# A new order of all engines for an attention-plus-feed-forward kernel, and five zero products at its start

## The chip, the cores and the metric

The kernel runs on one core of one Trainium2 chip. The metric is the device time of one execution in microseconds (us); smaller is better. Three runs of the kernel before gave 214.08, 215.25 and 216.29 us, so its median is 215.25 us.

## What is computed

The first stage is attention with a sliding window of 96 keys, eight global keys and a linear bias (a slope for each head); the second stage is a feed-forward layer with `h - tanh(h)` between its two products.

```python
# q, k, v: (4, 8, 768, 64) float32; n_global 8, n_local 96
scores = scale * np.matmul(q, k.transpose(0, 1, 3, 2))
is_global = pos[None, :] < n_global
is_local = (rel >= 0) & (rel < n_local)
dist = np.where(is_global & ~is_local, n_local, np.abs(rel))
scores = np.where(is_global | is_local, scores - slopes * dist, -1e9)
a = softmax(scores)                      # over the keys
x = (a @ v).transpose(0, 2, 1, 3).reshape(3072, 512)
h = x @ w_in                             # w_in 512 x 2048
out = (h - np.tanh(h)) @ w_out           # w_out 2048 x 512
```

## The kernel before

**Units.** The 3,072 rows are cut into 24 units of 128 queries (six to each of the four batches); one unit holds all eight heads. Units 0 to 3 are the first blocks of the four batches and see only their own 128 keys. Every later unit also needs the 128 keys before its own, and the eight global keys are copied into that block (`K` for the keys, `V` for the values).

**The order is written out by hand.** A long string `ORDER` (L17 to L65) lists all steps as words. Each word issues its instructions on one engine, and each engine runs its own words in the order of the string; nothing is reordered. A second string `HOMES` (L66 to L104) says which buffer or which of the eight PSUM banks each value lies in. A step waits for the data that it reads and for the last reader of the buffer that it writes, so both strings set the waits.

**The words of one unit u.** `lq.u`, `lk.u`, `lv.u` load q, k and v. For units 0 to 2, q and k come as float32: q over ACT's queue, k over SP's queue (`load_rows`, L292), and `cq.u`, `ck.u` cast them to bf16 on DVE (`/d`) or ACT (`/a`). All other loads go over POOL's queue. `T.u` transposes k and then q: on PE for units 0 to 6 (`a_T`, L305), with a copy from PSUM of each half (`Te.u.1` for k, `Te.u.0` for q, `a_Te`, L323); from unit 7 on as a DMA transpose issued by SP (`a_DT`, L332). `B.u` (only units 0 to 2) puts the bias and the mask into PSUM, two products of 512 columns (`bias`, L273). `S.n` are the score products (L347); from run 11 on, one `S` covers two blocks of one unit and one of a neighbour, so `S.11` needs the transposes of units 11 and 12. `E.u.o` is the exponential on ACT (L357), `M.u.o` the multiplication by the mask factors on DVE (L361), `AV.u` the product with v (L374), `R.u` the division by the row sum on DVE (L383), `X.u` the transpose of the result (PE for units 0 to 7, L394, with the copy `Xe.u`; later a DMA transpose by SP under the name `Xe.u`, L408).

**The masks.** DVE makes `dist`, `first` and `slopes` from an iota; `bm.m` are the products for the three masks (two of 512 columns each, L275) and `em.m` their exponential on ACT (L279).

**The feed-forward part.** Units are grouped: 0 and 1 alone, then three pairs (2 to 7), then four groups of four units. `m1.g.f` are the products with `w_in` for group g from chunk f on (L412), `th.g.f` the tanh on ACT, `g.g.f` the subtraction on DVE, `m2.u.c.a` a quarter of the products with `w_out` for unit u (L441), `ev.u` the copy of the result out of PSUM into one of four `ot` buffers (L450), and `st.u` the store (L453), on POOL's queue for units 0 to 20 and on SP's for the last three. `in.j` and `out.j` load the weights over POOL's queue: `in.0` and `in.1` two chunks of 128 columns each, `in.2` to `in.4` four each, `out.0` to `out.3` four chunks each.

**The helper `warm`** (L540) is one product of a zeroed tile with itself, 512 columns, into bank 7. The word `warm` does not occur in the order before, so no such product is issued.

The first words of PE in the order before are `bm.1 bm.0 B.1 T.1 B.0 T.0 S.1 T.3 B.2 S.0 T.2 S.3 AV.0 S.2 AV.1 X.0 T.4 X.1 AV.2 bm.2 m1.0.0 AV.3 X.2 m1.1.0 X.3 S.4`.

Of the kernel before, what the change touches and what calls it, by code (L numbers as in the profile page):

```python
# [17 lines left out]
lq.1 lk.1 zero rel ones.0 lq.0 lk.0 lq.3 slopes lq.2 lk.2 lk.3 dist table lv.0 turn bm.1 first ident lq.4 ones.1 bm.0  # L18
em.1 lk.4 cq.1/d ck.1/d B.1 lv.1 em.0 T.1 lv.2 B.0 cq.0/a ck.0/d in.1 Te.1.0/d Te.1.1/a T.0 in.0 S.1 Te.0.1/a Te.0.0/d
cq.2/a ck.2/d E.1.0 lv.3 T.3 B.2 in.2 Te.3.1/a Te.3.0/d S.0 lk.5 T.2 E.0.0 lq.5 S.3 Te.2.0/d Te.2.1/a AV.0 in.3 R.0  # L20
E.3.0 S.2 AV.1 out.0 X.0 R.1 E.2.0 T.4 out.1 M.3.0 X.1 Xe.0/a AV.2 bm.2 Te.4.1/d Xe.1/a out.2 m1.0.0 R.2 Te.4.0/a em.2
lv.4 AV.3 X.2 R.3 m1.1.0 Xe.2/a X.3 th.0.0 S.4 Xe.3/d th.1.0 in.4 g.0.0 m1.2.0 E.4.0 lk.6 g.1.0 m1.2.6 K.4 E.4.1 M.4.0
lq.6 m1.1.4 th.2.0 M.4.1 m1.2.2 th.1.4 g.2.0 m1.0.4 th.2.6 g.1.4 lv.5 th.2.2 T.5 g.2.6 m1.1.8 th.0.4 Te.5.0/d Te.5.1/a
g.0.4 m1.0.8 th.1.8 g.2.2 lq.10 S.5 th.0.8 g.1.8 m1.2.10 E.5.1 g.0.8 m1.2.8 K.5 th.2.10 M.5.1 m2.2.0.0 lv.6 E.5.0
g.2.10 m1.2.4 th.2.8 M.5.0 m2.1.0.0 g.2.8 th.2.4 m2.0.0.0 g.2.4 out.3 m2.2.0.1 lk.8 m2.2.0.2 m2.0.0.1 AV.4 lq.7
m1.1.12 V.4 lk.10 R.4 m1.2.14 th.1.12 lq.8 m1.0.12 g.1.12 th.2.14 lk.9 g.2.14 m1.2.12 th.0.12 lk.7 m2.1.0.1 g.0.12
th.2.12 lq.9 X.4 g.2.12 AV.5 Xe.4/a m2.1.0.2 R.5 T.6 V.5 lv.7 m2.0.0.2 Te.6.1/a Te.6.0/d lk.11 X.5 m2.2.0.3 Xe.5/a
m2.0.0.3 ev.2.0/a T.10 S.6 ev.0.0/a m1.3.10 T.8 E.6.1 K.6 m1.3.0 E.6.0 M.6.1 T.7 m1.3.2 th.3.10 M.6.0 m2.3.0.0 T.9
th.3.2 g.3.10 m1.3.4 th.3.0 g.3.2 m2.1.0.3 g.3.0 th.3.4 AV.6 g.3.4 ev.1.0/a m1.3.6 R.6 st.1.0 m1.3.12 lv.15 th.3.6 V.6
m2.3.0.1 g.3.6 lq.12 th.3.12 S.7 g.3.12 lv.8 m2.3.0.2 E.7.1 K.7 lv.17 m1.3.8 E.7.0 lk.13 M.7.1 X.6 m2.3.0.3 Xe.6/d  # L30
lv.10 th.3.8 M.7.0 S.8 ev.3.0/a st.0.0 g.3.8 AV.7 lv.9 E.8.1 m1.3.14 V.7 R.7 lq.11 E.8.0 m2.4.0.0 M.8.1 lq.18 X.7
th.3.14 m2.4.0.1 M.8.0 lk.12 Xe.7/a S.9 g.3.14 lq.13 AV.8 E.9.1 K.9 m2.4.0.2 lq.15 R.8 E.9.0 m1.4.6 lv.11 M.9.1 Xe.8
m2.4.0.3 M.9.0 th.4.6 lv.12 T.11 m1.4.8 g.4.6 ev.4.0/a S.10 T.12 th.4.8 AV.9 E.10.1 K.10 g.4.8 m1.4.0 T.13 R.9 E.10.0
m2.5.0.0 M.10.1 Xe.9 m1.4.4 th.4.0 V.9 M.10.0 m1.4.10 th.4.4 g.4.0 m2.5.0.1 th.4.10 g.4.4 AV.10 lq.14 g.4.10 m2.5.0.2
R.10 lv.16 m1.4.2 V.10 lv.13 Xe.10 S.11 th.4.2 lk.15 m2.5.0.3 g.4.2 E.11.0 lk.14 K.11 m1.4.12 K.12 ev.5.0/d E.11.1
st.4.0 m1.4.14 M.11.0 lk.17 th.4.12 M.11.1 m2.6.0.0 th.4.14 st.5.0 g.4.12 m2.6.0.1 E.12.0 g.4.14 AV.11 M.12.0 m2.7.0.0
R.11 m2.7.0.1 V.11 Xe.11 S.12 m2.7.0.2 T.15 E.12.1 m2.7.0.3 E.13.1 M.12.1 T.14 m2.6.0.2 ev.7.0/d E.13.0 AV.12 M.13.1
st.7.0 m2.6.0.3 lq.16 M.13.0 m1.5.7 R.12 ev.6.0/a lv.14 m1.5.6 th.5.7 V.12 Xe.12 lk.16 m1.5.1 g.5.7 th.5.6 lq.17 AV.13
g.5.6 th.5.1 lv.18 m1.5.3 R.13 lq.23 m1.5.0 th.5.3 g.5.1 Xe.13 lk.18 m1.5.11 g.5.3 th.5.0 m1.5.8 g.5.0 lq.19 th.5.11
S.13 g.5.11 lk.19 th.5.8 m1.5.4 g.5.8 E.14.0 T.16 K.14 m1.5.2 K.15 E.14.1 M.14.0 T.17 m1.5.9 th.5.4 M.14.1 m1.5.13  # L40
th.5.2 g.5.4 m1.5.14 E.15.0 g.5.2 m1.5.10 th.5.13 M.15.0 th.5.14 m1.5.5 g.5.13 T.18 th.5.10 g.5.14 m2.8.0.0 th.5.5
g.5.10 m1.5.15 th.5.9 g.5.5 AV.14 th.5.15 g.5.9 m2.8.0.1 T.19 V.14 R.14 m1.5.12 m2.8.0.2 g.5.15 Xe.14 th.5.12 S.14
g.5.12 m2.9.0.0 E.15.1 K.16 m2.8.0.3 E.16.0 M.15.1 m2.9.0.1 ev.8.0/d E.16.1 AV.15 M.16.0 st.8.0 m2.10.0.0 lv.19 R.15
m2.9.0.2 lk.23 V.15 Xe.15 M.16.1 S.15 lv.22 m2.9.0.3 E.17.1 K.17 lv.23 m2.10.0.1 ev.9.0/d E.18.0 st.6.0 m2.10.0.2
M.17.1 lq.22 E.17.0 M.18.0 m2.10.0.3 st.3.0 st.2.0 M.17.0 AV.16 lv.21 m2.11.0.0 V.16 T.23 R.16 lv.20 AV.17 m2.11.0.1
R.17 st.9.0 Xe.16 ev.10.0/a m2.11.0.2 lk.20 V.17 Xe.17 m1.6.0 st.10.0 lq.21 S.16 th.6.0 lq.20 m2.11.0.3 g.6.0 E.19.1
K.19 lk.21 m1.6.9 ev.11.0/d E.19.0 m1.6.6 M.19.1 th.6.9 M.19.0 m1.6.4 th.6.6 g.6.9 m1.6.3 E.18.1 lk.22 g.6.6 m1.6.15
th.6.4 M.18.1 th.6.3 AV.19 g.6.4 AV.18 th.6.15 g.6.3 m1.6.12 R.18 m1.6.2 th.6.12 V.19 Xe.18 m1.6.8 g.6.15 th.6.2 R.19
m1.6.7 th.6.8 g.6.12 Xe.19 m1.6.1 th.6.7 g.6.8 m1.6.11 th.6.1 T.20 g.6.7 m1.6.5 th.6.11 g.6.1 T.21 m1.6.10 g.6.11
th.6.5 g.6.2 m1.6.14 th.6.10 T.22 g.6.5 m1.7.12 th.6.14 g.6.10 m1.6.13 th.7.12 g.6.14 m1.7.1 g.7.12 th.6.13 m1.7.10  # L50
g.6.13 th.7.1 S.17 g.7.1 th.7.10 m2.13.0.0 g.7.10 E.21.0 K.21 m2.12.0.0 K.20 E.20.0 M.21.0 m2.13.0.1 E.20.1 M.20.0
m2.12.0.1 M.20.1 m2.13.0.2 AV.20 m1.7.14 V.20 R.20 m2.13.0.3 th.7.14 Xe.20 m1.7.9 g.7.14 ev.13.0/a m2.12.0.2 th.7.9
m2.12.0.3 g.7.9 S.18 ev.12.0/a m1.7.5 E.21.1 K.22 m2.14.0.0 E.22.0 M.21.1 m1.7.3 th.7.5 M.22.0 m1.7.2 th.7.3 g.7.5
# [13 lines left out]
mk.0:2,3 mk.1:0,1 mk.2:6,7 f32.0.k:3 kq.0:1 f32.0.q:2 f32.1.k:1 kq.1:0 f32.1.q:0 f32.2.k:5 kq.2:3 f32.2.q:4 v.0:0
v.1:1 kq.3:2 v.2:2 kq.4:4 v.3:3 v.4:4 kq.5:0 v.5:5 kq.6:1 v.6:6 kq.7:4 v.7:7 kq.8:3 v.8:9 kq.9:0 v.9:4 kq.10:2 v.10:11
kq.11:1 v.11:5 kq.12:2 v.12:6 kq.13:3 v.13:7 kq.14:1 v.14:9 kq.15:0 v.15:8 kq.16:3 v.16:0 kq.17:2 v.17:10 kq.18:4
v.18:4 kq.19:1 v.19:11 kq.20:2 v.20:7 kq.21:4 v.21:6 kq.22:3 v.22:5 kq.23:0 v.23:1 tr.0.0:1 tr.0.1:7 qk.0:1 s.0.0:2,3  # L70
p.0.0:1 av.0:2,3 x.0:0 xt.0:2 xT.0:0 tr.1.0:6 tr.1.1:0 qk.1:0 s.1.0:4,5 p.1.0:0 av.1:4,5 x.1:1 xt.1:1 xT.1:1 tr.2.0:4
tr.2.1:5 qk.2:3 s.2.0:6,7 p.2.0:3 av.2:4,5 x.2:2 xt.2:3 xT.2:2 tr.3.0:0 tr.3.1:1 qk.3:2 s.3.0:0,1 p.3.0:2 av.3:0,1
x.3:0 xt.3:5 tr.4.0:3 tr.4.1:0 qk.4:4 s.4.0:6,7 s.4.1:0,1 p.4.0:4 p.4.1:1 av.4:0,1 x.4:1 xt.4:0 xT.3:3 tr.5.0:7
tr.5.1:3 qk.5:5 s.5.0:0,1 s.5.1:6,7 p.5.0:3 p.5.1:0 av.5:4,5 x.5:2 xt.5:0 tr.6.0:7 tr.6.1:1 qk.6:6 s.6.0:4,5 s.6.1:0,1
p.6.0:1 p.6.1:2 av.6:4,5 x.6:0 xt.6:3 xT.4:1 qk.7:9 s.7.0:6,7 s.7.1:4,5 p.7.0:0 p.7.1:4 av.7:2,3 x.7:1 xt.7:6 qk.8:8
s.8.0:4,5 s.8.1:6,7 p.8.0:1 p.8.1:3 av.8:6,7 x.8:2 xT.5:0 qk.9:10 s.9.0:2,3 s.9.1:4,5 p.9.0:0 p.9.1:2 av.9:0,1 x.9:0
qk.10:7 s.10.0:6,7 s.10.1:2,3 p.10.0:1 p.10.1:4 av.10:0,1 x.10:1 qk.11:4 p.11.0:3 p.11.1:0 av.11:2,3 x.11:2 qk.12:5
# [30 lines left out]
def kernel(  # L108
# [11 lines left out]
    nc = tc.nc  # L120

    B, H, S, Dh = q.shape
    P = 128
# [352 lines left out]
    for u in range(NU):  # L476
        for j, (nm, src) in ((1, ("k", k)), (0, ("q", q))):
            if u < HW:
                h = ("f32", u, nm)
# [60 lines left out]
    def warm():  # L540
        nc.tensor.matmul(ps[:, 7, :], zero[:, 0, :], zero.to_broadcast([P, 4, P]), start=True, stop=True)

    done = set()
    with tc.manual_schedule(engines={PE, ACT, DVE, POOL, SP}):
        for word in ORDER.split():
            if word == "warm":
                warm()
                continue
# [40 lines left out]
```

## Time and profile before

| Quantity | Value |
|---|---|
| time, median of three runs | 215.25 us |
| time of the profiled execution | 215.35 us |
| its span, first to last instruction | 213.5 us |
| what lies around the span | 1.85 us |
| DVE busy | 130.4 us (61% of the span) |
| ACT busy | 120.5 us (56%) |
| POOL busy (mostly issuing DMAs) | 76.9 us (36%) |
| bytes moved by DMA | 27.55 MB, 129 GB/s on average |
| the product with `w_out` (L445) | 400 instructions, 91.2 us busy |
| the product with `w_in` (L420) | 576 instructions, 90.5 us busy |
| granted TensorE clock | 1.000 |

How to read it: an engine's busy time is the union of its instructions' times, without waits. The duration of one PE instruction includes its latency, and neighbours overlap in time, so a stretch of PE work is best read as the distance between starts. A line number is that of the instruction in the kernel; a helper such as the copy (L229 on ACT, L231 on DVE) serves many steps. A DMA's "landing" is counted from the issue to the last byte.

### The profile page before, as it was taken

The numbers are of one execution on the slowest core, as the hardware profiler recorded it, in microseconds if no ns is written. First come the engines' busy times: TensorE is split into PE (matmuls) and PEld (weight loads), VectorE is DVE, ScalarE is ACT, GpSimd is POOL, SyncE is SP. The second block draws the span as 40 slices with busy tenths as digits, with TensorE's granted clock in tenths as the row PEclk, the third lists the DMA queues.
The fourth block names the chain that finished last, engine by engine and source line by source line (L and its number), as shares of the span: only waits on it lengthen the run. The fifth ranks groups of instructions, "written<-read, shape, count | busy, mean of one in ns | idle before, by whom it ended". The sixth has DMA issues, their size and how long they took to land.

```text
span 213.5 us, 4492 instructions
## 1 busy us (share of the span) xinstructions
PE 204.6 (96%) x1796; PEld 117.2 (55%) x1796; DVE 130.4 (61%) x264; ACT 120.5 (56%) x179; POOL 76.9 (36%) x101
## 2 busy tenths in 40 slices
PE   4799999999999999999999999999999999999994
PEld 1467985857667665544555454444554444444442
DVE  7348883737787975789776498874567435611300
ACT  4579881557678474578445395673853335522422
POOL 8794435730995092780049830000010002002040
PEclk9999999999999999999999999999999999999999
DMA  5999999999999999999919999801021102002136
GB/s 164 243 177 189 208 198 175 179 157 194 128 177 150 141 154 216 181 151 137 175 53 166 195 206 150 147 3 25 0 78 25 25 3 98 0 0 98 52 116 228
DMA packets 100884, 27.55 MB, mean 129 GB/s; under 512 B 91840, under 2 KB 99264, under 8 KB 100864
## 3 DMA queue, kind: packets, MB, share of 16 engines
q0 software_dynamic: 72000, 18.36, 85.1%
q1 hardware_dynamic: 28048, 8.13, 23.5%
q10 hardware_dynamic: 816, 0.79, 1.2%
q8 instruction: 14, 0.23, 0.4%
q14 instruction: 6, 0.05, 0.1%
HBM read 27.26 MB, written 6.29 MB: 157 GB/s over the span
## 4 chain that ended last, share of the span: by engine, by line
PE 68%; issue 12%; DMA 10%; POOL 6%; DVE 1%; ACT 0%; SPq 0%; POOLq 0%; DVEq 0%; ACTq 0%
PE ps L420 30%; PE ps L445 28%; DMA qk<-kq 4%; POOL kq L297 3%; PE ps L352 3%; DMA f<-in_k_dram 3%; PE ps L378 3%; DMA out_dram<-ot 3%; POOL vb L297 2%; PE ps L398 1%; PE ps L317 1%; POOL out_dram L454 1%; PE ps L321 1%; PE ps L275 1%; PE ps L312 0%
## 5 line engine op out<-in xcount | busy, mean ns | idle before, releaser
L445 PE MATMUL ps<-w_out_bf,g 128*128 128x512 bf16 (+2 forms) x400 | 91.2, 371 | 0.0
L420 PE MATMUL ps<-xT,w_in_bf 128*128 128x512 bf16 (+2 forms) x576 | 90.5, 308 | 0.5 <-ACT ot L229 0.5
L436 DVE TENSOR_TENSOR g<-ps,th 128x512 bf16<-128x512 f32 x96 | 65.0, 688 | 38.7 <-ACT th L430 37.5
L430 ACT ACTIVATE th<-ps 128x512 f32<-128x512 f32 x96 | 56.7, 599 | 45.6 <-PE ps L420 44.8
L420 PEld LDWEIGHTS <-w_in_bf 128*128 128x128 bf16 x576 | 50.2, 98 | 33.9 <-issue 0.8
L445 PEld LDWEIGHTS <-g 128*128 128x128 bf16 x400 | 37.0, 98 | 38.0 <-DVE g L436 0.5
L454 POOL DMA_DIRECT2D out_dram<-ot x21 | 12.0, 576 | 106.3 <-ACT ot L229 86.5
L359 ACT ACTIVATE pr<-ps 128x1024 bf16<-128x1024 f32 x44 | 43.0, 1023 | 9.8 <-PE ps L352 9.8
L363 DVE TENSOR_TENSOR pr<-pr,mk 128x1024 bf16<-128x1024 bf16 x41 | 27.6, 687 | 8.0 <-ACT pr L359 7.9
L229 ACT COPY ot<-ps 128x512 f32<-128x512 f32 (+2 forms) x20 | 11.3, 565 | 26.6 <-PE ps L445 19.2
L297 POOL DMA_DIRECT2D vb<-in_v_dram x24 | 21.7, 912 | 5.1 <-DMA w_out_bf<-in_moe_w_out_dram 2.6
L297 POOL DMA_DIRECT2D kq<-in_q_dram x19 | 17.1, 911 | 12.4 <-DMA qk<-kq 8.2
L297 POOL DMA_DIRECT2D kq<-in_k_dram x19 | 17.1, 903 | 1.2 <-PE ps L352 0.5
L387 DVE TENSOR_TENSOR x<-ps,rden 128x512 bf16<-128x512 f32 x24 | 16.6, 692 | 0.8
L378 PEld LDWEIGHTS <-pr 128*128 128x128 bf16 x352 | 13.5, 98 | 4.2 <-issue 0.2
L378 PE MATMUL ps<-vb,pr 128*128 128x65 bf16 x352 | 14.8, 194 | 0.0
L352 PEld LDWEIGHTS <-qk 64*128 64x128 bf16 x352 | 10.2, 96 | 7.0 <-issue 6.3
L352 PE MATMUL ps<-qk 64*128 64x128 bf16 x192 | 10.1, 229 | 0.0
L231 DVE COPY vb<-vb 8x512 bf16<-8x512 bf16 x16 | 5.7, 356 | 5.9 <-PE ps L378 5.9
L275 PE MATMUL ps<-slopes,dist 128*128 128x512 bf16 x12 | 5.4, 587 | 3.1 <-DVE dist L242 3.1
L352 PE MATMUL ps<-qk,qk 64*128 64x128 bf16 x160 | 7.8, 217 | 0.0
L386 DVE RECIPROCAL rden<-ps 128x8 f32<-128x8 f32 x24 | 4.8, 199 | 2.8 <-PE ps L378 2.6
(41 smaller groups left out, 58.8 us busy)
## 6 DMA issues: line engine op xcount, KB each, us to landing
out_dram<-ot POOLq DMA_DIRECT2D x21, 256.0 KB, 2.8
vb<-in_v_dram POOLq DMA_DIRECT2D x24, 128.0 KB, 6.1
kq<-in_q_dram POOLq DMA_DIRECT2D x21, 128.0 KB, 6.9
kq<-in_k_dram POOLq DMA_DIRECT2D x21, 128.0 KB, 7.5
w_out_bf<-in_moe_w_out_dram POOLq DMA_DIRECT2D x4, 512.0 KB, 13.1
w_in_bf<-in_moe_w_in_dram POOLq DMA_DIRECT2D x3, 512.0 KB, 10.5
f<-in_q_dram ACTq DMA_DIRECT2D x3, 256.0 KB, 4.2
f<-in_k_dram SPq DMA_DIRECT2D x3, 256.0 KB, 6.9
```

Source lines behind the costliest of these rows:

```text
L229: nc.scalar.copy(out=out, in_=in_)
L297: eng(e).dma_start(out=dst, in_=rows_of(src, u).rearrange("h p d -> p h d"))
L352: nc.tensor.matmul(bank(("s", u, o), hh)[:, p * P : (p + 1) * P], buf(("qk", back[u] if o else u))[r, 1, p, :], buf(("qk", u))[r, 0, p, :] ...
L359: nc.scalar.activation(d, banks(("s", u, o), 0, 1), AF.Exp, bias=0.0, scale=scale)
L363: nc.vector.tensor_tensor(out=t, in0=t, in1=mk[:, mask_of(u, o)], op=ALU.mult)
L378: nc.tensor.matmul(t[:, h // (H // 2), h % (H // 2), :], buf(("p", u, o))[:, slot(h), :], buf(("v", back[u] if o else u))[:, h, 0 : Dh + 1 ...
L387: nc.vector.tensor_tensor(out=buf(("x", u)).rearrange("q (a h) d -> q a h d", a=2), in0=t[:, :, :, 0:Dh], in1=rden.to_broadcast([P, 2, H / ...
L420: nc.tensor.matmul(t[:, (f - f0) * n : (f - f0 + 1) * n], w_in_bf[j][:, c, fo : fo + P], x[:, c, 0:n], start=(c == 0), stop=(c == CD - 1),)
L430: nc.scalar.activation(h_view(buf(("th", g, f0)), g, m), h_view(bank(("h", g, f0)), g, m), AF.Tanh, bias=0.0, scale=1.0)
L436: nc.vector.tensor_tensor(out=buf(("g", g))[:, f0 : f0 + m, 0:n], in0=h_view(bank(("h", g, f0)), g, m), in1=h_view(buf(("th", g, f0)), g, ...
L445: nc.tensor.matmul(bank(part)[:, 0 : c1 - c0], buf(("g", g))[:, f, t * P : (t + 1) * P], w_out_bf[f // FJ][:, f % FJ, c0:c1], start=(f == ...
L454: eng(e).dma_start(out=out[turn_of[u] * P : (turn_of[u] + 1) * P, c0:c1], in_=buf(("ot", u))[:, c0:c1])
```

## The change

Both strings are written anew; the kernel's other code stays as it is, but for the helper, which now takes the bank from the word. Every step of before occurs once, as before. 798 words take the place of 793; the five new ones are `zero:7`, products of zeros into bank 7. Twenty-one copies change between DVE and ACT (among them `ev.5` to ACT and `ev.1`, `ev.2`, `ev.12` to DVE). All buffers and banks are dealt out anew; their number stays.

The opening, to the first products of the feed-forward part:

```diff
-lq.1 lk.1 zero rel ones.0 lq.0 lk.0 lq.3 slopes lq.2 lk.2 lk.3 dist table lv.0 turn bm.1 first ident lq.4 ones.1 bm.0
-em.1 lk.4 cq.1/d ck.1/d B.1 lv.1 em.0 T.1 lv.2 B.0 cq.0/a ck.0/d in.1 Te.1.0/d Te.1.1/a T.0 in.0 S.1 Te.0.1/a Te.0.0/d
-cq.2/a ck.2/d E.1.0 lv.3 T.3 B.2 in.2 Te.3.1/a Te.3.0/d S.0 lk.5 T.2 E.0.0 lq.5 S.3 Te.2.0/d Te.2.1/a AV.0 in.3 R.0
-E.3.0 S.2 AV.1 out.0 X.0 R.1 E.2.0 T.4 out.1 M.3.0 X.1 Xe.0/a AV.2 bm.2 Te.4.1/d Xe.1/a out.2 m1.0.0 R.2 Te.4.0/a em.2
-lv.4 AV.3 X.2 R.3 m1.1.0 Xe.2/a X.3 th.0.0 S.4 Xe.3/d th.1.0 in.4 g.0.0 m1.2.0 E.4.0 lk.6 g.1.0 m1.2.6 K.4 E.4.1 M.4.0
+lq.1 lk.2 zero rel ones.0 zero:7 dist lq.2 lk.1 zero:7 zero:7 slopes lq.0 lk.0 zero:7 table first turn bm.0 ident
+ones.1 lv.1 bm.2 em.0 cq.1/d bm.1 lk.3 ck.2/d em.2 lv.0 B.2 cq.2/d em.1 ck.1/d lq.3 zero:7 T.1 in.0 cq.0/d ck.0/a B.1
+Te.1.1/d Te.1.0/a lk.4 T.0 S.1 lq.4 Te.0.1/d Te.0.0/a T.2 E.1.0 lv.2 B.0 Te.2.1/d in.1 Te.2.0/a AV.1 S.0 R.1 lv.3
+E.0.0 T.3 in.2 AV.0 Te.3.1/d Te.3.0/a S.2 in.3 R.0 E.2.0 lq.5 X.0 S.3 lk.5 Xe.0/a X.1 T.4 E.3.0 Xe.1/d out.0 AV.2
+Te.4.1/d out.2 Te.4.0/a M.3.0 m1.0.0 out.1 R.2 AV.3 lv.4 th.0.0 m1.1.0 R.3 S.4 th.1.0 g.0.0 X.3 E.4.0 X.2 g.1.0 lv.5
+m1.0.4 Xe.2/d Xe.3/a m1.1.4 K.4 M.4.0 th.0.4 m1.2.6 E.4.1 g.0.4 lk.8 m1.2.2 th.1.4 M.4.1 lk.6 m1.0.8 th.2.6 g.1.4
...
```

The words of two queues after it, taken out of the string in their order. SP's transposes, units 8 to 13:

```diff
-T.10 T.8 T.7 T.9 Xe.8 T.11 T.12 T.13 Xe.9 Xe.10 Xe.11 T.15 T.14
+T.8 T.7 T.9 T.10 T.13 T.11 Xe.8 T.12 Xe.9 Xe.10 Xe.11 T.14 T.15
```

POOL's loads and stores from the fourth `w_out` part on, to the load of `lv.11`, and again around the stores of units 8 to 10:

```diff
-out.3 lk.8 lq.7 lk.10 lq.8 lk.9 lk.7 lq.9 lv.7 lk.11 st.1.0 lv.15 lq.12 lv.8 lv.17 lk.13 lv.10 st.0.0 lv.9 lq.11 lq.18
-lk.12 lq.13 lq.15 lv.11 lv.12 lq.14
+out.3 lv.6 lq.8 lq.7 lq.10 lk.7 lk.9 lk.10 lq.12 lv.7 lq.11 lv.8 lv.10 lv.17 lv.12 lq.13 lq.18 lk.13 st.0.0 lk.11 lv.9
+lv.15 lk.12 st.1.0 lq.15 lq.14 lv.11
...
-st.8.0 lv.19 lk.23 lv.22 lv.23 st.6.0 lq.22 st.3.0 st.2.0 lv.21 lv.20 st.9.0 lk.20 st.10.0
+st.8.0 lv.23 lk.22 lv.19 lv.21 lv.20 st.9.0 st.6.0 lv.22 lq.21 st.2.0 st.10.0
```

The `ot` buffers of the units 6 to 10, and the helper:

```diff
-ot.6:1 ot.7:2 ot.8:2 ot.9:2 ot.10:1
+ot.6:2 ot.7:2 ot.8:0 ot.9:0 ot.10:0
...
-    def warm():
-        nc.tensor.matmul(ps[:, 7, :], zero[:, 0, :], zero.to_broadcast([P, 4, P]), start=True, stop=True)
+    def warm(b):
+        nc.tensor.matmul(ps[:, b, :], zero[:, 0, :], zero.to_broadcast([P, 4, P]), start=True, stop=True)
...
-            if word == "warm":
-                warm()
+            if word.startswith("zero:"):
+                warm(int(word[5:]))
                 continue
```

## The prediction

> **What bounds the kernel now.** I read the page first, then the chain of waits, PE's waits, and the DMA issues of the first 3 us. The page's busy line and PE's slices:
>
> ```profile
> PE 204.6 (96%) x1796; PEld 117.2 (55%) x1796; DVE 130.4 (61%) x264; ACT 120.5 (56%) x179; POOL 76.9 (36%) x101
> ...
> PE   4799999999999999999999999999999999999994
> ```
>
> PE is full from the third slice to the last; the same PE work lies in both orders, so time can come only from the opening, from stalls between, and from the tail. All that PE waited for on other engines (in total, times, longest):
>
> ```profile
> PE ps L275 <- DVE dist L242: 3.1, 1, 3.1
> PE ps L317 <- DVE kq L231: 1.4, 1, 1.4
> PE ps L420 <- ACT ot L229: 0.5, 1, 0.5
> PE ps L398 <- DVE x L387: 0.4, 1, 0.4
> PE ps L321 <- DVE qk L231: 0.3, 1, 0.3
> ```
>
> Only 0.5 us of this lies behind the opening. The chain of waits (start, us, what):
>
> ```profile
> 1.54 6.92 DMA f<-in_k_dram
> ...
> 8.49 0.44 DVE kq L231
> ...
> 8.97 1.05 PE ps L317 x8
> ...
> 11.93 0.97 PE ps L275 x2
> ...
> 14.94 0.57 PE ps L378 x8
> ...
> 17.89 0.24 PE ps L378 x8
> 18.13 0.43 PE ps L275 x2
> ...
> 66.83 7.73 DMA qk<-kq
> ...
> 113.67 5.81 DMA out_dram<-ot
> ...
> 119.55 0.59 ACT ot L229
> ```
>
> Two things are to be seen. First, SP's second load (k of unit 0) lands at 8.46 and holds PE until 8.97. Second, the same products take twice the time early on: two of 512 columns 0.97 us at 11.93 and 0.43 at 18.13; eight of 65 columns 0.57 at 14.94 and 0.24 at 17.89. The change falls near 15.4, although the granted clock reads 1.000 throughout. Call the two rates slow and fast. PE ran 10 us in the opening at the slow rate, so some 5 us are lost there, beside 5.2 us of waits. The landings of SP's loads, for issues in 0 to 1.45, 1.45 to 2.2 and 2.2 to 3 us (the last figure is the median):
>
> ```profile
> f<-in_k_dram SPq DMA_DIRECT2D x1, 256.0 KB, 4.2
> ...
> f<-in_k_dram SPq DMA_DIRECT2D x2, 256.0 KB, 5.6
> ...
> f<-in_k_dram SPq DMA_DIRECT2D x2, 256.0 KB, 7.3
> ```
>
> The first lands at 0.74+4.2 = 4.9. The second took 6.92, so the third took 2x7.3-6.92 = 7.7 and lands at about 2.3+7.7 = 10.0. ACT's three landed at about 4.2, 5.6 and 8.6.
>
> **The opening with the loads as they were.** SP's order becomes k of unit 2, 1, 0. T.1 needs the second, so it starts at 8.97, where T.0 was; before it started at 5.64. What covers the time until then: the mask products can't start at 3.1, since `first` now stands behind the slopes: iota done 1.2, dist 1.0 (three rows at L240 to L242), slopes 0.8, first 0.4, hence 3.5. Eight slow products of 512 columns at 0.43 reach 6.95. Before 8.97, PE so does bm.0, bm.2, bm.1 and B.2, against bm.1, bm.0, B.1, B.0 and T.1 before: one T less.
>
> The five zero products: 5x0.43 = 2.2 us at the slow rate. Four lie in 1.0 to 2.7, inside the 3.1 us in which PE waited for dist; the fifth ends at 7.4, inside the wait for k. I take nothing for them; if k of unit 1 landed before 7, the fifth would cost 0.2 to 0.4.
>
> ACT's words are ck.0, Te.1.0, Te.0.0, E.1.0, in this order. ck.0 waits for SP's third load at 10.0, and Te.1.0, which S.1 needs, is queued behind it: ck.0 to 10.6, Te.1.0 to 11.2. That is the new wait, and all of S.1, E.1.0 and AV.1 stand behind it.
>
> What follows hangs on when PE turns fast. Durations: T 0.96 slow, 0.48 fast (eight of L317); S 0.54 and 0.25; AV 0.57 and 0.24; X 0.22 fast; exponential 1.02 (L359); copies 0.60 on ACT, 0.69 on DVE; R 0.95 (L386, L387); M 0.68 (L363); m1 0.89. The mark is the end of the same work: T, S, AV, X of units 0 to 4 or 0 to 3, all masks, m1.0.0 and m1.1.0. Before, it is the end of S.4 at 21.75 in the chain; in the new order the end of X.2.
>
> Middle case, fast from 13.3: T.1 8.97 to 9.93, B.1 10.79, T.0 11.75, S.1 12.29, T.2 13.25, B.0 13.7, AV.1 (E.1.0 12.4 to 13.4) 13.9, S.0 14.2, T.3 14.8. Now ACT and DVE bound: E.0.0 ends 15.27, AV.0 15.55, S.2 15.8; R.0 starts behind Te.3.1 and ends 16.55, X.0 16.8, S.3 17.05, X.1 17.3, T.4 17.9, AV.2 18.1, m1.0.0 19.0 (its weights landed at 16.5 before, behind as many bytes). M.3.0 ends 19.3 (E.3.0 behind Xe.0 on ACT, then DVE), AV.3 19.6, m1.1.0 20.5, S.4 21.0; R.2 and R.3 follow M.3.0 on DVE until 21.1, X.3 21.35, X.2 21.6. Against 21.75: a gain of 0.15.
>
> The same walk, fast only from 15.4 as in the profile: S.0 ends 15.2, E.0.0 16.27, R.0 17.6, M.3.0 20.4, R.3 22.2, X.2 22.7: a loss of 0.95. Fast before 8.97: T.0 waits for ck.0 until 10.65, S.1 11.5, AV.1 13.1, E.0.0 14.47, R.0 15.75, M.3.0 18.5, X.2 20.7: a gain of 1.05.
>
> When does PE turn fast? Before, PE was busy from 3.1 to 7.5, 4.4 us on end, and was still slow at 8.97; then it was busy without a gap from 10.87 and fast from 15.4. Now it is busy from 1.0 to 2.7, from 3.5 to 7.4, and without a gap from 8.97, two us earlier than 10.87. If the 4.5 us (10.87 to 15.4) carry over, it turns at 13.5: the middle case, which I take. The Trainium skill (TensorE: Matmul & The Clock Gate, Part 1) says that a busy window of some 3.4 us opens the gate and that the window runs free of the kernel. The trace agrees so far as 4.4 us did not suffice once. By the rule, the turn would come 3.4 to 6.8 us behind 8.97, at 12.4 to 15.8, or, in the luckiest phase, before T.1.
>
> **Behind the opening.** The PE words are the same; their order costs nothing unless a wait arises. Copies changed between ACT and DVE (0.60 against 0.69) lie under a full PE: nothing. Three places are near.
>
> Weights: in.4 stands behind lv.5, lk.8 and lk.6 now, three loads of about 0.8 us each, so it lands near 35.5+2.4 = 38 (before 20.28+15.2). Summing PE's words from 21.6, m1.0.12 needs it at 39.4: margin 1.4. out.1 stays at about 32 (before out.2, 16.85+15.2) against 34.0. I take nothing; up to 1 if late.
>
> Transposes: S.11 before started at 75.41, and T.12 landed at about 68.44+6.9 = 75.3, no margin. Now T.13 and T.11 go ahead of Xe.8, T.12 behind it. By the count of POOL's issues lk.12 is issued at about 62.9 (62.5 before) and T.12 at 68.3, with two transposes less beside it: landing 72.5 to 75 against a need at 76.3. lq.14 waits for T.11 on POOL (8.2 us before), and lv.11 is now queued behind it: issued about 72.5, landed 78 against AV.11 at 80.5. Nothing; 1 to 2 if T.9, which lq.18 awaits, is late.
>
> Stores: units 8, 9 and 10 share one ot buffer. st.9 follows five loads on POOL, as st.6 did at 113.67 when it took 5.81 us. By PE's words m1.6.0 then waits about 0.75, where before it waited 0.5; with the median store (2.8) not at all. So -0.5 to +0.6; I take +0.2, nearest to the 5.81 row. The tail keeps its last words: nothing.
>
> **Sum.** From the profiled 215.35: -0.15 +0.2 = 215.4. The median of before is 0.1 lower, so 215.3 in its terms, in effect no change.
>
> **Rivals.** About 1% (2.15 us) is what a measurement of this kernel tells from no change; the three runs alone span 2.2.
>
> PE fast before T.1: 215.25-1.05+0.2 = 214.4. For it: 3.9 us of masks on end behind 1.7 us of zeros. Against: 4.4 us didn't do it before. The page's rule gives this in one phase of several. With SP's loads landing like ACT's (5.6, 8.6), S.1 comes 1.35 earlier still: 213.0, faster than 1%. The trace shows SP's later than ACT's.
>
> PE slow until 15.4: 216.4, the phase of the profiled run repeated.
>
> Slower: SP's third load. S.1 follows its landing at one for one through ck.0 and Te.1.0 on ACT. At 11.5 (other loads of k over POOL took 7.4 and more) and with a late turn the loss is 1.5+0.95+0.2: 217.9. It decides from a landing behind 10.4, where T.0 starts to wait. Against it: with v first on POOL, nothing larger competes than before.
>
> Slower behind the opening: T.12, in.4 or lv.11 late, a stall of 2 to 3: 217.3 to 218.3. For it: T.12 had no margin at 75.3 before, and in.4 has 1.4. Against: the counts above.
>
> Zeros that don't count as activity, so that the change doesn't do what it says, end in the slow and middle cases, since neither uses them: 215.3 to 216.4.
>
> **How the numbers follow.** Middle 0.36, slow until 15.4 0.20, fast before T.1 0.16, that with early loads 0.07, third load late 0.09, stall behind 0.12. The likeliest gives 215.3; its own range is 214.4 to 216.4. The range of 8 in 10 takes in the gains down to 213.0 and part of the losses: 213.0 to 217.8. Faster by over 1% (under 213.1): early loads and a part of the fast case, 0.11. Slower (over 217.4): both slower rivals with a little more, 0.22. Within: 0.67.
>
> **What would show it.** The zero products at 1.0 to 2.7; T.1 near 9.0; S.1 near 12, behind ck.0 and Te.1.0; AV.0 waiting for ACT and X.0 for DVE, some 0.5 and 0.8 us; eight products of 65 columns turning from 0.57 to 0.24 between 12.4 and 15.8; X.2 ending between 20.7 and 22.7; one wait of m1.6.0 for ev.10 below 1 us. PE waits over 1 us at L352, L420 or L378 behind 25 us would prove me wrong, and so would T.1 before 7.5.

## The result, and the profile after

| | before | after |
|---|---|---|
| median of the runs | 214.76 us (214.08 to 216.29, four runs) | 217.55 us (217.16 to 218.24, four runs) |
| profiled execution | 215.35 us, span 213.5 | 217.85 us, span 216.1 |
| mean granted clock of it | 1.000 | 0.992 |

The fourth run of the kernel before, 214.28, brought its median down to 214.76. The ratio after to before is 1.0146, 95% interval 1.0110 to 1.0181: the kernel after is slower, by over 1%. The profiled executions differ by 2.6 us of span, and three marks place them. The end of the opening (the end of S.4 before, of X.2 after) went from 21.75 to 23.82, +2.07. From there to the end of PE's work it took 188.63 before and 188.91 after, +0.28. From PE's end to the end of the span it took 3.12 and 3.37, +0.25. So four fifths of the loss lie in the first 24 us.

The page of the kernel after, its busy line, PE's slices and the granted clock (slices of 5.4 us):

```profile
PE 204.3 (95%) x1801; PEld 116.5 (54%) x1801; DVE 131.6 (61%) x269; ACT 118.1 (55%) x174; POOL 76.8 (36%) x101
...
PE   7387999999999999999999899999999999999993
...
PEclk9969999999999999999999999999999999999999
```

PE does the same 204 us of work. Its first slice is fuller than before (7 against 4, the zero products and the earlier masks), its second far emptier (3 against 7), its third and fourth emptier too (8 and 7 against 9 and 9), and in the third slice the granted clock falls, which it did nowhere in the profile of before. What PE waited for on other engines in the kernel after, above 0.5 us (in total, times, longest):

```profile
PE ps L318 <- DVE kq L232: 3.2, 1, 3.2
PE ps L318 <- ACT kq L230: 1.1, 1, 1.1
PE ps L542 <- DVE vb L272: 1.0, 1, 1.0
PE ps L421 <- ACT ot L230: 0.7, 1, 0.7
PE ps L399 <- DVE x L388: 0.7, 1, 0.7
PE ps L276 <- DVE dist L250: 0.6, 1, 0.6
PE ps L379 <- ACT pr L360: 0.6, 1, 0.6
```

The first two are T.1 waiting for the cast of SP's second load, and T.0 waiting for the cast of SP's third; before, one such wait cost 1.4. The old wait of 3.1 for `dist` did not vanish: it became 1.0 (the zeroed tile) plus 0.6 (`dist`), and the time gained so was waited out in front of T.1 instead. What SP's second and third load took from issue to landing in the kernel after (the issues alone that lie in 1.70 to 1.95 us and in 2.65 to 3 us; the last figure is the time):

```profile
f<-in_k_dram SPq DMA_DIRECT2D x1, 256.0 KB, 7.4
...
f<-in_k_dram SPq DMA_DIRECT2D x1, 256.0 KB, 8.6
```

Before, the same two took 6.9 and 7.7. Issued at 1.54 and 2.42, they landed at 8.96 and 11.03 here; before, it was 8.46 and about 10.1. The chain of waits of the kernel after runs through the third (start, us, what):

```profile
2.42 8.60 DMA f<-in_k_dram
11.05 0.63 ACT kq L230
11.72 1.04 PE ps L318 x8
12.76 0.54 PE ps L353 x8
13.30 0.96 PE ps L318 x8
14.27 0.79 PE ps L276 x2
```

T.0 takes 1.04 here, although T.1 took 0.62 two microseconds earlier (from its start to that of the next step 0.97, against 0.46): PE was fast and became slow again. The windows of the kernel after say when (stretch in us; busy time of PE, PEld, DVE, ACT and POOL with instructions; then the granted clock, the DMA share and GB/s):

```profile
11.00:11.50 0.50, 0.00 (x0) 0.00 (x0) 0.50 (x2) 0.45 (x1) 0.01 (x1) 0.95 1.51 195
11.50:14.50 3.00, 2.78 (x26) 2.11 (x27) 1.38 (x3) 2.36 (x5) 2.38 (x4) 0.50 1.71 183
14.50:15.00 0.50, 0.50 (x6) 0.24 (x5) 0.14 (x1) 0.39 (x1) 0.50 (x1) 0.64 1.45 197
15.00:25.00 10.00, 8.39 (x178) 7.15 (x176) 7.93 (x17) 7.35 (x11) 6.12 (x8) 1.00 1.56 193
```

The clock was halved for 3.4 us, from about 11.45 to 14.85, right behind the emptiest stretch of PE (1.05 us busy in 8 to 11).

### The profile page after: what moved, and what is told of

Its sections match the earlier page's. It is cut to its first block, busy times and chain, and to the rows that moved or that the text cites. A ratio compares the mean times of both kernels' runs of the same rounds, so it can differ in the third digit from the quotient of the medians.

```text
span 216.1 us, 4513 instructions
## 1 busy us (share of the span) xinstructions
PE 204.3 (95%) x1801; PEld 116.5 (54%) x1801; DVE 131.6 (61%) x269; ACT 118.1 (55%) x174; POOL 76.8 (36%) x101
## 4 chain that ended last, share of the span: by engine, by line
PE 66%; issue 11%; DMA 10%; POOL 8%; ACT 1%; DVE 1%; SPq 1%; POOLq 0%; ACTq 0%; DVEq 0%
PE ps L421 30%; PE ps L446 28%; POOL kq L298 4%; DMA f<-in_k_dram 4%; DMA qk<-kq 4%; PE ps L353 3%; PE ps L379 3%; POOL vb L298 3%; DMA out_dram<-ot 2%; PE ps L399 1%; POOL out_dram L455 1%; PE ps L318 1%; SPq L295 1%; ACT pr L360 0%; PE ps L313 0%
## 5 line engine op out<-in xcount | busy, mean ns | idle before, releaser
L446 PE MATMUL ps<-w_out_bf,g 128*128 128x512 bf16 (+2 forms) x400 | 90.1, 371 | 0.0
L360 ACT ACTIVATE pr<-ps 128x1024 bf16<-128x1024 f32 x44 | 43.1, 1024 | 12.1 <-PE ps L353 10.4
L230 ACT COPY ot<-ps 128x512 f32<-128x512 f32 (+2 forms) x18 | 10.1, 561 | 20.3 <-PE ps L446 14.4
L353 PEld LDWEIGHTS <-qk 64*128 64x128 bf16 x352 | 10.0, 95 | 6.3 <-issue 5.1
L353 PE MATMUL ps<-qk 64*128 64x128 bf16 x192 | 9.7, 222 | 0.0
L232 DVE COPY ot<-ps 128x512 f32<-128x512 f32 x7 | 4.8, 692 | 5.3 <-PE ps L446 4.3
L353 PE MATMUL ps<-qk,qk 64*128 64x128 bf16 x160 | 7.8, 217 | 0.0
L232 DVE COPY vb<-vb 8x512 bf16<-8x512 bf16 x16 | 4.9, 304 | 3.1 <-PE ps L379 3.1
```

The lines of the kernel that those rows point to most:

```text
L230: nc.scalar.copy(out=out, in_=in_)
L353: nc.tensor.matmul(bank(("s", u, o), hh)[:, p * P : (p + 1) * P], buf(("qk", back[u] if o else u))[r, 1, p, :], buf(("qk", u))[r, 0, p, :] ...
L360: nc.scalar.activation(d, banks(("s", u, o), 0, 1), AF.Exp, bias=0.0, scale=scale)
L446: nc.tensor.matmul(bank(part)[:, 0 : c1 - c0], buf(("g", g))[:, f, t * P : (t + 1) * P], w_out_bf[f // FJ][:, f % FJ, c0:c1], start=(f == ...
```

## The experiments

Two theories stood against each other. **Landings**: SP's loads land later because of what else is loaded, and T.1, T.0 and all behind them follow. **Clock**: the zero products turn PE fast early, and the waits undo it. The rival to both was that the new order costs time behind the opening. "Mark" is the end of the opening as above. Durations and marks come from one profiled execution of each kernel, ratios from repeated runs of it against runs of the kernel before on the same chip; they are not the quotients of the medians given here. Many edits below move words of one queue; the diffs show that queue's words.

**The clock: filling the wait, and leaving the zeros out.** To the kernel after, ten more zero products ahead of T.1 (the first edit); its five zeros taken out (the second); and, to the kernel before, ten zeros, four ahead of the masks and six behind B.0 (the third).

```diff
-B.2 zero:7 T.1 B.1 T.0
+B.2 zero:7 zero:7 zero:7 zero:7 zero:7 zero:7 zero:7 zero:7 zero:7 zero:7 zero:7 T.1 B.1 T.0
```

> The changed kernel with ten more zero products ahead of T.1, so that the 3.3 us in which PE waited for k of unit 1 are mostly filled. The granted clock should then stay at 1.00 (it fell to 0.50 from 11.45 to 14.85). Theory A (the clock falling back is the larger part of the 2.1 us lost in the opening): X.2 ends 1 to 1.5 earlier than 23.8, the time is some 1.2 us below the changed kernel's 217.5. Theory B (the loads of k for units 1 and 0 come too late, and ACT and DVE set the pace behind them): clock at 1.00, but X.2 ends at most 0.5 earlier, time 217.0 to 217.5.

> The changed kernel without its five zero products, all else as it is. If the zeros are what turned PE fast at 4.6 us, the masks run slow here (0.43 us a product) until about 7 and the turn comes only at 12 to 16, with T.0, S.1 and T.2 slow as they were in the changed kernel. Theory A and B both say that the zeros gain nothing in the changed order: time within 0.5 us of 217.5. If the zeros cost by themselves, it is faster by more than 0.5; if they helped, slower by more than 0.5.

> The kernel before, with its own order, plus four zero products ahead of the masks and six behind B.0, in the wait for k of unit 0. The clock should turn to fast near 4.6 and hold, since no wait of PE is left over 2 us. Then T.0, S.1, T.3, B.2, S.0, T.2 run at the fast rate from 9 on: S.4 ends at 19.8 to 20.5 in place of 21.75, time 213.0 to 213.8 against 214.8 for before. Rival: the opening of before hangs on loads (v of unit 1 at 13.0, w_in at 16.5) and on ACT and DVE anyway, so S.4 ends no earlier than 21 and the time is within 0.5 us of before.

With the wait filled: 216.78 us, ratio 1.0091 (1.0056 to 1.0126). The clock stayed at 1.00 (in all ten runs its mean is 0.997 or more), T.0 started at 11.38, hardly earlier than after's 11.72, and the mark came at 22.54 against 23.82. But the whole gain of 1.28 us was lost again at one place. Two lines of PE's waits in this kernel:

```profile
PE ps L379 <- DMA vb<-in_v_dram: 1.5, 1, 1.5
...
PE ps L318 <- ACT kq L230: 0.8, 1, 0.8
```

The first is AV.11, waiting for `lv.11` until 82.82; in the kernel after it waited 0.16 for the same load, until 82.79. That is a second floor: whatever the opening gains, AV.11 starts at about 82.8. The span still ended 0.8 us earlier, but that arose behind AV.11, where m1.6.0 had waited 0.71 for a copy into `ot` in the kernel after and did not wait here.

Without zeros: 216.9 us, 1.0085 (1.0040 to 1.0129). The masks ran slow, T.1 started at 9.97, and PE turned fast near 15.9, about as late as in the kernel before; this profile is of the slowest of the ten runs (218.88). Its interval overlaps that of the kernel after, so the zeros are not shown to cost or to gain anything in this order. In the order before, ten zeros made all its products fast from about 4.6 us on and the mark earlier by 0.45 us (21.30 against 21.75), and the ratio was 0.9984 (0.9946 to 1.0021): no difference that can be told. There the waits for loads took over: m1.0.0 waited 0.58 for `w_in`, AV.3 0.75 for v.

**The order of SP's and ACT's loads.** In the kernel after, units 1, 0, 2 again, as before (with the casts of unit 2 behind `Te.0.0`); in the kernel before, the new order.

```diff
-lq.1 lk.2 lq.2 lk.1 lq.0 lk.0
+lq.1 lk.1 lq.0 lk.0 lq.2 lk.2
```

> The changed kernel with the loads of before again: SP takes k of units 1, 0, 2, ACT takes q of units 1, 0, 2, and the casts of unit 2 go behind Te.0.1 on DVE. Theory B: T.1 starts near 6.5 in place of 9.6, T.0 near 9.1 in place of 11.7, S.1 near 9.8 in place of 12.7, X.2 ends some 2 us earlier, time 215.2 to 215.7; the wait of PE splits into two of under 3 us, so the clock may stay up too. Theory A alone: if the clock falls all the same, under 0.8 us are won, 216.7 or more.

> The kernel before with one part of the change alone: SP takes k of units 2, 1, 0 and ACT q of units 1, 2, 0; all engines keep the order of before. If the order of the k loads is what costs, T.1 starts near 9 (5.6 before) and T.0 near 10.5 to 11, S.4 ends 1.5 to 2.5 later than 21.75, and the time is 1.5 to 2.5 above before, 215.8 to 216.8, since no lv.11 hides it. If it costs nothing by itself, within 0.5 of before.

The first gave 217.93, ratio 1.0137 (1.0062 to 1.0211), no better than after; the second 216.09, 1.0038 (1.0001 to 1.0075). With k of unit 1 first, T.1 started at 7.25, but k of unit 0 then came second and took 7.6 us: T.0 waited 1.40 for it and T.2 1.27 for the third. The mark came at 21.92, 1.9 earlier than in the kernel after, as expected, but AV.11 then waited 1.85 for `lv.11`, and the median was no better. In the second, T.1 started at 8.25 and the mark came at 22.72, 1.0 later than before. So the order of the three loads moves the opening by a microsecond or two in a profile; a gain from it in the median is not shown.

**The second floor.** `lv.11` moved ahead of `lq.15` and `lq.14` on POOL, alone, with the filled wait, and with the old order of SP's loads:

```diff
-lq.15 lq.14 lv.11
+lv.11 lq.15 lq.14
```

> The changed kernel with one word moved: the load lv.11 goes ahead of lq.15 and lq.14 on POOL's queue, so that it no longer stands behind the 9.1 us in which lq.14 waits for the transpose T.11. Theory C (behind the late opening lies a second floor, lv.11, which held AV.11 at 82.6 to 82.8 in three kernels whose openings ended 2 us apart): in this kernel the opening is as late as that floor, so AV.11 starts only 0.2 earlier and the time stays within 0.4 of the changed kernel, 217 to 217.6. Rival: lv.11 is the main cost by itself, then 215.5 or less.

> The kernel with ten more zeros ahead of T.1, and lv.11 ahead of lq.15 and lq.14. The opening ends near 22.5 (1.3 earlier than the changed kernel) and nothing holds AV.11: it starts near 81.3, time 215.7 to 216.5, below the 216.8 of the zeros alone. Rival: no gain, since the wait moves to another load or store.

> Both parts undone: the loads and casts of the opening in the order of before, and lv.11 ahead of lq.15 and lq.14. Theory C with the late loads: X.2 ends near 21.9, AV.11 starts near 80.7 without a wait, the time is some 2 us below the kernel with the loads alone, 215.0 to 215.9. Rival (another wait takes the place of lv.11, or the loss lies elsewhere): AV.11 near 82 or a new wait of over 1 us behind it, 216.7 or more.

| edit | median | ratio (95%) | mark | AV.11 starts |
|---|---|---|---|---|
| `lv.11` alone | 217.81 | 1.0121 (1.0055 to 1.0187) | 23.44 | 82.08, no wait |
| with the filled wait | 216.04 | 1.0064 (1.0026 to 1.0101) | 21.65 | 81.34, no wait |
| with old load order | 217.13 | 1.0127 (1.0080 to 1.0175) | 20.19 | no wait |

Alone it changes nothing that can be told, since the opening is late enough to hide it. With the filled wait the AV.11 wait of 1.5 us is gone, and the transposes behind it show as the next floor (two waits at L353, 0.75 and 0.51). The profile of the third kernel is the best execution of its ten (214.16; they reach 219.42): its second load took 6.0 us, not 7.6.

**Late transposes or late loads.** That third kernel's spread had two explanations: the wait for transposes that its profile shows (0.48 at S.11), or loads that land late in other executions. One run put the loads of units 11 and 12 ahead of those of unit 13 on POOL and their transposes ahead on SP; one took the same kernel again for another profile.

```diff
-T.8 T.7 T.9 T.10 T.13 T.11 Xe.8 T.12
+T.8 T.7 T.9 T.10 T.11 Xe.8 T.12 T.13
```

> The kernel with the loads of before in the opening and lv.11 moved, and a third part undone: units 11 and 12 are loaded and transposed ahead of unit 13 again (lq.13, lq.18, lk.13 behind lk.12 on POOL, T.13 behind T.12 on SP). The kernel without this part ran at 214.16 at best but 217.1 in the median. Theory D (its slow executions are held by T.12 and S.11, which had 0.5 us of wait even in its best one): median 215.0 to 215.8 and a narrower spread. Theory E (its slow executions are held in the opening, by loads that land late): median within 0.6 of 217.1.

> The kernel with the loads of before and lv.11 moved, once more, for a profile of an ordinary execution. Theory D: a wait of 1 us or more at S.11 or AV.11, with X.2 near 20 to 21. Theory E: X.2 ends at 22 or later, with T.0 and T.2 waiting for their loads, and no wait over 0.6 behind 26 us.

The first removed the wait at S.11 and the median was no better: 217.71, 1.0118 (1.0060 to 1.0175). The second's profiled execution, at 218.68 us, had its second load land after 8.5 us: T.0 waited 2.79 for it, the clock fell, and the mark came at 23.92, against 20.19 in the earlier profile of the very same kernel. Of the 4.5 us between the two spans (212.4 and 216.9), 3.7 lie in the opening; S.11 waited 0.67 here, hardly more than 0.48. So the late transposes fell as a cause, and the landings stood.

**The queue on ACT.** The prediction's new wait was ck.0, queued ahead of `Te.1.0` on ACT. Here `Te.1.0` goes ahead of ck.0, `Te.1.1` ahead of cq.0, and S.1 ahead of T.0, with `lv.11` early; and the kernel after was run again unchanged.

```diff
-T.1 cq.0/d ck.0/a B.1 Te.1.1/d Te.1.0/a T.0 S.1
+T.1 B.1 Te.1.1/d Te.1.0/a cq.0/d ck.0/a S.1 T.0
```

> The changed kernel with lv.11 moved, and the wait undone that the prediction named: ACT copies Te.1.0 ahead of ck.0, DVE Te.1.1 ahead of cq.0, and PE does S.1 ahead of T.0. S.1 should start near 10.8 in place of 12.3 to 12.7, E.1.0 behind ck.0 near 11.7 in place of 13.3. T.0 still waits for SP's third load. If the queue behind ck.0 is what costs, X.2 ends 0.8 to 1.5 earlier, time 216.2 to 216.8 against 217.8; if T.0 and what follows it set the pace, under 0.4 is won.

> The changed kernel as it is, beside the others on one chip, for a spread: 217 to 218.2 as in its first four runs, with the clock falling back in the opening and X.2 ending at 23 to 24.

216.35 us, 1.0096 (1.0063 to 1.0129): S.1 moved ahead to 11.36, but T.0 followed at 11.90 and the mark stayed at 23.48. The queue on ACT gives at most a part. The kernel after again: 216.08 in four runs, 1.0110 (1.0032 to 1.0187), the same loss. Its profile caught earlier landings (6.2 and 7.4 us), and the clock fell all the same. The timeline of PE in that run (start, us; in brackets the wait ahead):

```profile
8.27 0.62 PE L318 MATMUL ps<-turn,kq 128*128 128x128 bf16 x8 [0.83 <-DVE kq L232]
8.73 0.59 PE L276 MATMUL ps<-slopes,dist 128*128 128x512 bf16 x2
10.49 0.64 PE L318 MATMUL ps<-turn,kq 128*128 128x128 bf16 x8 [1.17 <-ACT kq L230]
11.06 0.60 PE L353 MATMUL ps<-qk 64*128 64x128 bf16 x8
11.60 1.04 PE L318 MATMUL ps<-turn,kq 128*128 128x128 bf16 x8
```

T.1 and T.0 take 0.62 and 0.64, T.2 takes 1.04: the clock halves at 11.0 behind waits of 0.83 and 1.17 us.

**POOL's opening.** What is loaded beside SP's and ACT's loads at that time is POOL's opening. Its order is varied next: the kernel after with `lv.11` early and POOL's first nine loads in the order before; that with the old order of SP's and ACT's loads too; and the kernel before with after's nine loads.

```diff
-lv.1 lk.3 lv.0 lq.3 in.0 lk.4 lq.4 lv.2 in.1
+lq.3 lk.3 lv.0 lq.4 lk.4 lv.1 lv.2 in.1 in.0
```

> The changed kernel with lv.11 moved and with POOL's first nine loads in the order of before (lq.3 lk.3 lv.0 lq.4 lk.4 lv.1 lv.2 in.1 in.0). Theory F (v first and w_in early on POOL's queue hold up SP's k loads): SP's second and third load land near 8.2 and 10.0, as with before's queue, in place of 7.8 to 9.5 and 9.8 to 11.4; the median falls by 0.6 to 1.2, to 215.2 to 216.6. Theory G (they scatter by themselves): landings as before the edit, median 216.5 to 217.8.

> Both: k and q loads of SP and ACT and POOL's first nine loads in the order of before, lv.11 moved, the orders of PE, ACT and DVE still those of the change (but for the casts of unit 2). Theory F: T.0 starts near 9.2, X.2 ends near 21, median 214.3 to 215.5, near before. Theory G, or if the orders of PE, ACT and DVE cost by themselves: median 216 or more.

> The kernel before with one part of the change alone: POOL's first nine loads in the order of the changed kernel (lv.1 lk.3 lv.0 lq.3 in.0 lk.4 lq.4 lv.2 in.1). Theory F: SP's second load lands near 9 in place of 8.2, S.4 ends up to 1 later, the median is 0.6 to 1.2 above before. Theory G: within 0.4 of before; T.3, which needs lq.3, may then cost a little by itself.

The first is 214.97 (ten runs, 214.38 to 217.09), 1.0053 (1.0014 to 1.0092); the second 215.04, 1.0054 (1.0013 to 1.0094); the third 215.40, 1.0046 (1.0013 to 1.0078). The interval of the first lies below that of the kernel after (1.0110 to 1.0181) and overlaps that of `lv.11` early alone (1.0055 to 1.0187); by the middle values more than half of the loss is gone. In the third half a per cent is put on, and its interval is clear of 1. SP's second and third load in the first of them, in the same two windows as above:

```profile
f<-in_k_dram SPq DMA_DIRECT2D x1, 256.0 KB, 5.8
...
f<-in_k_dram SPq DMA_DIRECT2D x1, 256.0 KB, 7.0
```

1.6 us less each than in the kernel after. Over all profiles, the six with POOL's order of before gave 5.6 to 6.9 for the second load (mean 6.25) and 7.0 to 8.1 for the third (7.47); the twelve with after's order gave 5.9 to 8.5 (7.12) and 7.3 to 9.0 (8.10). The ranges overlap. The means differ by 0.87 and 0.63, and the third run of this group is a miss for its profile: its second load took only 6.0, its third 8.1, and T.3 waited 0.74 each for its own two loads, which now stand further back.

**Which part of POOL's opening, and both causes at once.** From the kernel with POOL's old opening: v first again, `w_in` last; v last, `w_in` fifth again; and POOL's old opening with eight more zeros ahead of T.1.

```diff
+lv.1 lk.3 lv.0 lq.3 lk.4 lq.4 lv.2 in.1 in.0
+lq.3 lk.3 lv.0 lq.4 in.0 lk.4 lv.1 lv.2 in.1
```

> The kernel after with lv.11 ahead of lq.15 and lq.14 on POOL, and with in.0 (w_in) back behind lv.2 on POOL; v stays first (lv.1, lk.3, lv.0, lq.3, lk.4, lq.4, lv.2, in.1, in.0). Theory 'v first' (v's 256-byte rows, first in POOL's queue, hold back SP's second and third loads): they land near 8.7 and 10.7 as in the kernel after, the opening ends near 23.4, ratio about 1.012. Theory 'w_in early' (what holds them back is in.0 as fifth load): they land near 7.9 and 9.9, opening near 22, ratio about 1.005. If both parts count half, about 1.009.

> The kernel after with lv.11 ahead of lq.15 and lq.14, and with v back behind unit 3's and 4's loads on POOL while in.0 stays fifth (lq.3, lk.3, lv.0, lq.4, in.0, lk.4, lv.1, lv.2, in.1). Theory 'v first': SP's second and third loads land near 7.9 and 9.9, opening near 22, ratio about 1.005, and a wait of AV.1 on its v of 0.3 to 1 us. Theory 'w_in early': landings near 8.7 and 10.7, ratio about 1.012.

> The kernel with POOL's first nine loads in the order of before and lv.11 ahead (the run that gave 1.0053), with eight more zero products of the seventh kind ahead of T.1. Theory 'landings and clock': both causes of the late opening are then met: the granted clock stays at 1.00 from the first slice on, T.0 starts near 10, X.2 ends near 20.8 against 21.75 before, and the ratio is 0.997 to 1.003. Rival 'order behind T.0' (the new order of all engines costs time of its own, whatever the landings and the clock): X.2 ends near 21.5 or later with T.0 near 10, and the ratio stays at 1.004 to 1.006.

v first: 217.05, 1.0094 (1.0048 to 1.0140); `w_in` fifth: 217.20, 1.0108 (1.0037 to 1.0179). By the middle values each part alone brings most of the loss back, with landings of 7.7 and 8.3 us in the one, 7.4 and 8.7 in the other; both intervals overlap the 1.0014 to 1.0092 of POOL's old opening, so this is likely and not shown. Neither theory came out as expected, for only both put back together helped. The last one: 215.16, 1.0011 (0.9978 to 1.0044), no difference from before that can be told. All waits of PE above 0.6 us in it:

```profile
PE ps L276 <- DVE dist L250: 1.0, 1, 1.0
PE ps L542 <- DVE vb L272: 1.0, 1, 1.0
PE ps L379 <- ACT pr L360: 0.8, 2, 0.6
PE ps L399 <- DVE x L388: 0.7, 1, 0.7
```

The waits for loads are gone and the granted clock is 1.00 in every slice. Its mark missed what was expected (22.26, not 20.8), because PE turned fast only near 9.3, so that the zeros ran on until 10.2 and pushed T.0 to 11.10, where its data would have let it start near 10.2. The step from 1.0053 to 1.0011 lies inside the intervals, so the worth of the fill on top of POOL's order is not shown; that both together are level with before is.

**What the profiles say together.** From the start of T.0 to the mark, the new order takes one of three lengths, by how long the clock was down:

| kernel | granted clock, 10 to 18 us | T.0 starts | mark | T.0 to mark |
|---|---|---|---|---|
| after | 0.50 for 3.4 us | 11.72 | 23.82 | 12.10 |
| after, again | 0.50 for 3.4 us | 10.49 | 22.66 | 12.17 |
| after, `lv.11` early | 0.50 for 3.4 us | 11.28 | 23.44 | 12.16 |
| wait filled | 1.00 | 11.38 | 22.54 | 11.16 |
| wait filled, `lv.11` early | 1.00 | 10.48 | 21.65 | 11.17 |
| POOL's old opening | 1.00 | 10.09 | 21.31 | 11.22 |
| that, wait filled | 1.00 | 11.10 | 22.26 | 11.16 |
| v first again | 0.50 for 6.8 us | 11.43 | 24.20 | 12.77 |
| `w_in` fifth again | 0.50 for 6.8 us | 11.86 | 24.77 | 12.91 |

So in these profiles a fall of 3.4 us costs about 0.95 us, one of 6.8 us 1.6 to 1.75. The opening of the kernel after is then a sum: against POOL's old opening (21.31), T.0 starts 1.63 later and the clock takes 0.88 more (12.10 against 11.22), together the 2.51 by which its mark is later. And in that execution, whose two loads took 1.1 and 0.7 us less than in the profile of before, the new opening ends at 21.3, only 0.4 before the old one.

The mean granted clock is on record for every run, not only for the profiled ones. A fall of 3.4 us lowers the mean of a span of some 215 us by 0.008, to 0.992. All eight runs of the kernel after stand at 0.992 or lower, and so do all four with `lv.11` early alone, but only one of twenty in the two kernels with the wait filled, one of ten with POOL's old opening, and none of ten with both. In the halves it is eight of ten (v first) and two of four (`w_in` fifth). Two things follow that the profiles alone hide. POOL's old opening kept the clock up in nine of ten runs without any fill, so the fill had little left to mend there. And the kernel before is not free of falls: 45 of its 105 runs in these comparisons stand at 0.992 or lower, though its profile shows none, and nine of ten do when it gets after's nine loads on POOL, though that kernel's profile is of the tenth. A mean does not say where in the run the clock fell.

## Why the prediction was wrong

The forecast was "in effect no change", 215.3; the profiled execution took 217.85, 2.45 above the 215.4 of the sum. The median of 217.55 lies inside the range of 8 in 10, near its upper end of 217.8, and outside the 214.4 to 216.4 of the likeliest case. The opening of that case ended X.2 at 21.6, and measured was 23.82. Of these 2.22 us, 0.93 lie ahead of T.0 (start at 10.79 in the walk, 11.72 measured) and 1.29 behind its start (10.81 in the walk, 12.10 measured).

- **The failed step ahead of T.0: the landings (0.93).** The walk put T.1 at 8.97 and ck.0 behind a landing "at 10.0", the times of before. They were taken as fixed while the same change gave POOL another opening. They landed 0.5 and 1.0 later; T.1 started at 9.61 and T.0 at 11.72, where the walk had 10.79. The sentence that let this stand is the one against the third rival, "with v first on POOL, nothing larger competes than before": the bytes are the same, their order was not, and over all profiles POOL's new opening goes with landings later by 0.87 and 0.63 us on average.
- **The failed step behind T.0: the length of the walk (1.29).** The fast case had X.2 at 20.7 for a T.0 at 10.65, 10.05 us. Measured with a fast clock it is 11.16 to 11.22, so some 1.1 us were missing in every case. About 0.4 of that lies ahead of X.0: R.0 ended 5.10 us behind the start of T.0 in the walk, and 5.48 with the filled wait and `lv.11` early. From X.0 on the walk counted products at their bare durations and left out waits such as the 0.36 of m1.0.0 on `Te.4.1`. Even with the landings of before, the fast case would have ended near 21.8, level with 21.75. The other 0.2 is the clock: for slow products the middle case had allowed 0.76 (10.81 less 10.05), and the fall cost some 0.9.
- **That rival came true, its price in part by luck.** A third load behind 10.4, passed on through ck.0, with slow products, is what was measured; it had a chance of 0.09. Its 217.9 is also what came, but it counted a landing at 11.5 (11.03 came) and a PE that turns fast late, where PE turned early and became slow again. Its opening loses 1.5+0.95 = 2.45, and 2.07 were measured; behind the opening it had 0.2, and 0.28+0.25 came.
- **The turn of the clock.** The middle case had PE slow until 13.3. With zeros ahead of the masks PE was fast by the end of T.1 in all sixteen profiles, near 4.6 us in the kernel after, so "fast before T.1", held for unlikely because 4.4 us did not suffice before, was the right half of that rival. What no case held was that PE could be made slow again, as it was for 3.4 us from 11.45 on. That the middle case came near with its price for slow products is luck. By the rule that the prediction quoted from the Trainium skill (TensorE: Matmul & The Clock Gate, Part 1: The HAM clock gate), a window of some 3.4 us that runs free, the turn behind a start at 1.0 lies at an estimated 4.4 to 7.8, and all these profiles agree but one: with POOL's old opening and the wait filled, PE turned only near 9.3, 5.4 us behind the start of the masks. The same section says that an idle window takes the clock back. The 3.4 us at 0.50 agree with it in length; but in the kernel after run again PE was busy 1.56 of the 3 us ahead of the fall, so a wait need not fill the window.
- **Right.** S.1 stood behind ck.0 and `Te.1.0` (12.69, "near 12"); AV.0 waited 0.55 on ACT and X.0 0.70 on DVE, against "some 0.5 and 0.8"; the one wait of m1.6.0 for ev.10 was 0.71, against 0.75; no wait of PE above 1 us lies behind 25 us.
- **Right for the wrong reason: `lv.11`.** "Issued about 72.5, landed 78": it was issued at 77.4 and landed at 82.74, because `lq.14` waited for T.11's transpose, which took 7.63 us and ended at 76.0. It cost 0.16 only because the opening was late; with an earlier opening it cost 1.5 to 1.9. T.12 likewise: forecast at 72.5 to 75, it landed at 77.30, and S.11 waited for it (0.75 and 0.48) only where the opening was earlier.
- **The tail** was taken as unchanged and took 0.25 more; no experiment was aimed at it.

Open: why POOL's loads should hold SP's back when v comes first or `w_in` comes fifth, each alone. The profile shows the landings, not how the 16 engines shared their time between the queues. Also open is how much of the loss the clock and how much the landings cost in the median, since the intervals of POOL's old opening with the fill and without it overlap. None of the versions was faster than the kernel before by more than its interval.

## What to carry to other kernels

When a change reorders the loads of one queue, the landings on the other queues are not constants to be carried over: give each a range from several executions, and let the first product wait only for a load with room in it. Zeros that turn TensorE fast early gained nothing that can be told here, neither in the order before nor in the new one; where they are used, the first real products have to follow without long waits, and a filled wait should end when the load lands, not behind it. A gain early in the kernel has to be walked to the next late load: here AV.11's swallowed all of the filled wait's 1.28 us until its load was moved. And a profile shows one execution: the granted clock of all runs told more about the falls than any single trace.

## What the runs showed of the hardware

- The granted clock reads 1.00 in the first slices of the kernel before, while its products run at half rate until 15.4; it shows a fall, not the state at the start.
- Four products of zeros from 1.0 us on and the masks behind them made PE fast by the end of T.1 in all sixteen profiles that have them: near 4.6 us in the kernel after, and at the latest near 9.3, after 5.4 us of products on end (POOL's old opening, wait filled). Without zeros PE turned near 15.4 in the kernel before and near 15.9 in the new order.
- With just these five zeros in the new order the clock fell again in seven of twelve profiles, for 3.4 us in four of them and for 6.8 us in three; it fell in none of the three with the wait filled. Waits as in the runs with the old load order (1.40 and 1.27 in one, 2.13 and 1.15 in another) did not always bring it down.
- Over whole runs, the mean granted clock of the kernel before was 0.992 or lower in 45 of 105, of the kernel after in eight of eight.
- A load of 256 KB issued at the same 1.54 us landed after 5.6 to 8.5 us, and after 6.0 and 8.5 in two executions of one and the same kernel.
